# The first stage of an attention and gated-MLP kernel, written in another order: masks, transposes, product copies and weight steps

## Chip, core and metric

One core of a Trainium2 chip. The metric is device time in microseconds of one launch: 820.15 us in the median of three runs (817.03 to 821.88) for the kernel before. Engine names: TensorE (PE; PEld is its weight load), VectorE (DVE), ScalarE (ACT), GpSimd (POOL), SyncE (SP), which issues the DMAs.

## What is computed

Attention with a decay term for 8 batches of 8 heads (576 tokens, 64 per head), then a gated MLP on the joined heads:

```python
scores = scale * np.matmul(q, k.transpose(0, 1, 3, 2))
decay = cum[:, :, :, None] - cum[:, :, None, :]          # cum: running sum of log f
scores = np.where(causal, -1000000000.0, scores + decay)
attn = softmax(scores)
x = np.matmul(attn, v)                                   # heads joined: (8, 576, 512)
h = np.maximum(x @ w_in, 0.0); u, v = h[..., :512], h[..., 512:]
v_n = (v - mean) / sqrt(var + 1e-06)
out = (u * (w_spatial @ v_n + b_spatial)) @ w_out
```

## The kernel before

Two heads make a pair; a batch has four pairs (PPB = 4), there are 32 in all. Of a head's 576 query rows, four blocks of 128 are handled by head; the last 64 rows of both heads share one tile, the tail. For a pair, TensorE computes scores; DVE (`lowest`, line 279) adds the decay table, finds the row minimum and writes the weights' exponents; ACT (line 310) takes the exponential with a row sum; POOL (`share`, line 287) scales by the reciprocal; TensorE transposes the weights (line 379 by head, 389 for the tail); ACT and DVE copy the transposes out of PSUM (line 370); and TensorE multiplies them with v (line 417). That last step is called the product. Its result is split into two float32r parts: xh by ACT (line 426), xl by DVE (line 427).

The kernel has two stages. The first (`first`) does the attention of batch 0 and, beside it, brings in the weights: w_in comes as 64-bit numbers in four blocks, each going through a DMA (line 120), one ACT operation (125), five DVE operations (127 to 133), a POOL addition (135), an ACT cast (137) and a POOL subtraction (138); `go(blocks, n)` takes one of these steps. A w_spatial slice (`go(spaces, n)`) is a DMA (151), then an ACT cast (153) and a POOL subtraction (154). In the second stage the MLP of one batch runs beside the attention of the next, and a planner places its instructions; it also converts the other half of w_in and w_out.

In the first stage the order on every engine is the written one: a loop after `period` ties each instruction to the one before it on its engine. `period(P)` overlaps the scores of pair X = P + 1 with the transposes and the product of pair P, for P = -1 to 3; `y` is true from P = 0 on. `prep(P)` issues a pair's five loads on SP (q and k, the decay tables dk of both heads, the tail's tables dt); `mask(P)` is six POOL selections on these tables; `prep_v` loads v once the product before has read the old one. Scores use PSUM banks 0 to 3, the product banks 4 and 5, transposes two buffers `tp`. `leave()` finishes the product of the pair before: the xh and xl copies. `keep_warm` runs matmuls on zeros.

Of the kernel before, what the change touches and what calls it, by code (L numbers as in the profile page):

```python
# [8 lines left out]
F32 = mybir.dt.float32  # L9
# [11 lines left out]
S = 576  # L21
# [10 lines left out]
def f32(ap):  # L32
    return ap.bitcast(F32)
# [3 lines left out]
def attn_gmlp_kernel(ctx: ExitStack, tc: tile.TileContext, qk, v, f, w_in, w_sp, b_sp, w_out, out):  # L37
# [163 lines left out]

    freed, banks = {}, []

    def bank(n):

        t = PS['s'].tile([128, 512], F32, name="sc", tag=f"sc{n}")
        banks.append(n)
        return t

    def in_one_piece(jobs, needs=()):  # L210
# [37 lines left out]
    def mask(P):  # L248

        _, dk, dt = tab[P]  # L250
        for h in range(2):
            two = dk[h][:, 256:768].rearrange("p (c w) -> p c w", w=256)[:, :, 0:128]
            G.affine_select(out=two, in_=two, compare_op=ALU.is_ge, fill=-8.0 * BIG, base=0,
                            pattern=[[0, 2], [-1, 128]], channel_multiplier=1)
            G.affine_select(out=dk[h][:, 640:896].rearrange("p (c w) -> p c w", w=128),
                            in_=dk[h][:, 0:256].rearrange("p (c w) -> p c w", w=128), compare_op=ALU.is_ge,
                            fill=-8.0 * BIG, base=0, pattern=[[0, 2], [-1, 128]], channel_multiplier=1)
            p = slice(64 * h, 64 * h + 64)
            G.affine_select(out=dt[p, TL:S], in_=dt[p, TL:S], compare_op=ALU.is_ge, fill=-8.0 * BIG, base=0,
                            pattern=[[-1, 64]], channel_multiplier=1)  # L260

# [20 lines left out]
    def share(P, t, r):  # L282

        if PPB < P < 2 * PPB:
            A.activation(t, t, AF.Copy, scale=r)
        else:
            G.tensor_scalar(out=t, in0=t, scalar1=r, scalar2=1.0, op0=ALU.mult, op1=ALU.mult)  # L287
# [82 lines left out]
        copied.setdefault(P, []).append(by(out, ps))  # L370
        nev[0] += 1

    def turn_block(P, h, c, by=None):

        tt, _ = turn(P)
        n = 512 - 128 * c
        tp = PS['t'].tile([128, 512], F32, name="tp")
        for i in range(c, NB):
            T.transpose(out=tp[:, (i - c) * 128:(i - c + 1) * 128],  # L379
                        in_=tt[h][:, TOFF[i] + 128 * c:TOFF[i] + 128 * c + 128], identity=ident)  # L380
        return lambda by=None: evac(P, e_tile(P)[:, h, EOFF[c]:EOFF[c] + n], tp[:, 0:n], by)
# [26 lines left out]
    def attend(P, xh, xl):  # L408

        vt, e = vts[P], es.pop(P)  # L410
        xb = 4 if P < PPB else 0
        x0, x1 = bank(xb), bank(xb + 1)
        jobs = []

        def product(x, s0, q0, q1, c, h, end):
            e0 = EOFF[c] - 128 * c
            return lambda: T.matmul(x[64 * h:64 * h + 64, q0 - s0:q1 - s0], vt[:, c, h, :],  # L417
                                    e[:, h, e0 + q0:e0 + q1], start=c == 0, stop=c == end)

        for c in range(NB + 1):  # L420
            for x, s0, q0, q1, end in ((x1, 256, max(256, 128 * c), S, NB), (x0, 0, 128 * c, 256, 1)):
                jobs += [product(x, s0, q0, q1, c, h, end) for h in range(2) if c <= end]
        in_one_piece(jobs, copied.pop(P))
        yield 2950
        for ps, s0, n in ((x0, 0, 256), (x1, 256, 320)):
            last[P, s0 // 256] = A.copy(xh[:, s0:s0 + n], ps[:, 0:n])  # L426
            freed[xb + s0 // 256] = V.tensor_tensor(out=xl[:, s0:s0 + n], in0=ps[:, 0:n], in1=f32(xh[:, s0:s0 + n]),  # L427
                                               op=ALU.subtract)
        yield 0
# [10 lines left out]
    def first(ws):  # L440

        blocks, spaces, pending = {}, {}, []

        def leave():
            for g in pending:
                for _ in g:
                    pass
            pending.clear()

        def go(d, n):  # L450
            if n in d:
                next(d[n], None)

        def period(P):

            X = P + 1
            y = P >= 0
            qk_t, dk, dt = tab[X]
            tt, tl = turn(X)
            nm = wk.tile([128, 2, 4], F32, name="nm", tag="nm8", bufs=2)  # L460
            sa = wk.tile([128, 2, 3], F32, name="sa", tag="sa", bufs=2)
            sb = wk.tile([128, 2, 1], F32, name="sb", tag="sb", bufs=2)
            nt = wk.tile([128, 4], F32, name="nm", tag="nm", bufs=6)
            st = wk.tile([128, 4], F32, name="sm", tag="sm", bufs=6)

            def low(i, at):
                for h in range(2):
                    weigh(X, i, h, tt[h], dk[h], at, nm[:, h, i:i + 1], sb[:, h, 0:1] if i == 3 else sa[:, h, i:i + 1])

            def inverse(s_):  # L470
                V.tensor_scalar(out=s_, in0=s_, scalar1=1.0e-9, scalar2=None, op0=ALU.add)
                V.reciprocal(s_, s_)

            def spread(i, s_):
                for h in range(2):
                    t = tt[h][:, TOFF[i]:TOFF[i] + 128 * (i + 1)]
                    share(0, t, s_[:, h, 0:1])

            def two(h, c):
                if y:  # L480
                    a = turn_block(P, h, c)
                    b = turn_block(P, h, c + 1)
                    a(A.copy)
                    b(V.tensor_copy)

            at = score_piece(X, qk_t, (0, 1, 2))
            if y:
                if P + 2 <= PPB:
                    list(prep(P + 2))
                go(blocks, P + 2)  # L490
            else:
                keep_warm(6)
            low(2, at)
            leave()
            go(spaces, P)
            two(0, 0)
            low(1, at)
            go(blocks, P)
            low(0, at)
            go(blocks, X)  # L500
            two(0, 2)
            at = score_piece(X, qk_t, (3,))
            if not y:
                keep_warm(6)
            two(1, 0)
            inverse(sa)
            low(3, at)
            for i in (2, 1, 0):
                spread(i, sa[:, :, i:i + 1])
            two(1, 2)  # L510
            tails = []
            for j in range(2):
                sc = bank(2 + j)
                mm(sc[:, 0:288], qk_t[:, TL:640], qk_t[:, 640 + 288 * j:928 + 288 * j], True, True)
                tails.append(sc)
            banks.clear()
            for j in range(2):
                k0 = 288 * j
                freed[2 + j] = lowest(tl[:, k0:k0 + 288], tails[j][:, 0:288], dt[:, k0:k0 + 288], nt[:, j:j + 1])
            V.tensor_tensor(out=nt[:, 2:3], in0=nt[:, 0:1], in1=nt[:, 1:2], op=ALU.min)  # L520
            inverse(sb)
            spread(3, sb)
            A.activation(tl[:, 0:S], tl[:, 0:S], AF.Exp, bias=nt[:, 2:3], scale=-1.0, accum_out=st[:, 0:1])
            if y:
                a, b = (turn_tail(P, *k) for k in TAILS)
                a(A.copy)
                b(V.tensor_copy)
            go(blocks, X)
            inverse(st[:, 0:1])
            share(0, tl[:, 0:S], st[:, 0:1])  # L530
            if P + 2 <= PPB:
                mask(P + 2)
            go(blocks, X)
            if y:
                pending.append(product(P))
                next(pending[0])
                if X < PPB:
                    prep_v(X)
            go(spaces, X)

        for c in range(NJ):
            blocks[c] = load_first(ws, c)
        for c in range(NB + 1):
            spaces[c] = load_space(ws, c)
        traced = nc.cur_bb.bb.instructions
        start = len(traced)
        rows, qk0, qk1 = decay_rows(), prep(0), prep(1)
        next(rows)
        next(qk0)
        next(blocks[0])  # L550
        next(rows)
        next(qk0)
        prep_v(0)
        list(qk1)
        next(blocks[1])
        warm.append(PS['t'].tile([128, 512], F32, name="tp"))
        keep_warm(30)
        mask(0)
        for P in range(-1, PPB):
            period(P)  # L560
        leave()
        was = {}
        for i in list(traced)[start:]:
            if i.engine in was:
                tc.add_manual_dep(i, was[i.engine].name, mybir.DependencyInfo(
                    mybir.DependencyClass.NoSync, mybir.DependencyReason.DATA), reason="order")
            was[i.engine] = i
        go(spaces, NB)
# [210 lines left out]
```

## Time and profile before

| | |
|---|---|
| median of three runs (lowest to highest) | 820.15 us (817.03 to 821.88) |
| the profiled execution, its own time | 819.35 us |
| its span, first to last instruction | 817.2 us |
| TensorE matmul, busy | 769.7 us (94%) |
| DVE / ACT / POOL, busy | 430.5 / 417.2 / 368.1 us |
| mean granted TensorE clock | 0.974 |
| chain that ended last: TensorE's share | 69% |

The profile is of one execution. Shares over the whole span are a mean over two stages: the first ends at some 101.6 us, when TensorE starts on the MLP of batch 0. The rows below are therefore taken from stretches. Matmuls are pipelined and their ends are modelled; an idle time stands in brackets ahead of the instruction that ended it, with what released it. A clock of 1.0 is 2.4 GHz, 0.5 is 1.2 GHz.

### The profile page before, as it was taken

The page shows a single profiled execution, that of the slowest core. Times are in us where ns is not written, and L with a number is a line of the kernel's source. Part 1 is how long each engine was busy: PE and PEld are TensorE (multiplying, and loading weights), DVE is VectorE, ACT ScalarE, POOL GpSimd, SP SyncE. Part 2 cuts the span into 40 slices and gives each one's busy share as a digit, 9 for nine tenths or more (in the row PEclk, how much of TensorE's full clock was granted, in tenths as well). Part 3 has the DMA queues.
Part 4 walks back from the last instruction along what each step waited for, and adds up shares of the span by engine and source line. Part 5 has one row for each costly group of instructions (what it writes and reads, how often), then busy time and mean ns, then how long its engine had stood idle before and what let it go on. Part 6 is the DMA issues. An engine that isn't in the chain of part 4 may idle for free.

```text
span 817.2 us, 14547 instructions
## 1 busy us (share of the span) xinstructions
PE 769.7 (94%) x4922; PEld 608.2 (74%) x4922; DVE 430.5 (53%) x1502; ACT 417.2 (51%) x1127; POOL 368.1 (45%) x686
## 2 busy tenths in 40 slices
PE   6676788989999999999999999999999999999997
PEld 2344467768788877887788777888788778878896
DVE  2566779855454446545564536544464446544322
ACT  2555548775565446544564446544564446543331
POOL 1566566433544436333554436334554445433231
PEclk9689899999999999999999999999999999999999
DMA  7544434422333333222332333312332332211001
GB/s 197 166 134 139 131 112 146 134 73 80 98 94 95 120 119 93 94 60 82 115 94 94 120 107 100 96 47 92 120 95 94 120 103 72 85 31 43 27 1 65
DMA packets 34764, 79.43 MB, mean 97 GB/s; under 512 B 4225, under 2 KB 8321, under 8 KB 34690
## 3 DMA queue, kind: packets, MB, share of 16 engines
q1 hardware_dynamic: 34370, 77.98, 31.1%
q8 instruction: 39, 0.64, 0.3%
q10 hardware_dynamic: 320, 0.52, 0.2%
q14 instruction: 35, 0.29, 0.1%
HBM read 68.73 MB, written 9.75 MB: 96 GB/s over the span
## 4 chain that ended last, share of the span: by engine, by line
PE 69%; issue 5%; DVE 4%; POOL 3%; DMA 2%; ACT 2%; POOLq 0%; DVEq 0%; ACTq 0%
PE ps L226 39%; PE sc L417 8%; PE tp L379 7%; PE sc L299 7%; PE sc L226 5%; PE tp L226 2%; DMA out_dram<-o 1%; POOL gl L680 1%; PE tp L389 1%; DVE tt L279 1%; ACT tt L310 1%; POOL tt L287 1%; ACT gh L679 1%; DVE w L130 0%; DMA dt<-rows_d 0%
## 5 line engine op out<-in xcount | busy, mean ns | idle before, releaser
L310 ACT ACTIVATE tt<-tt,nm 128x128 f32<-128x128 f32 (+2 forms) x240 | 133.7, 558 | 120.5 <-DVE nm L279 118.0
L287 POOL TENSOR_SCALAR tt<-tt,sm 128x128 f32<-128x128 f32 x192 | 99.7, 537 | 110.8 <-DVE sm L326 110.8
L379 PE MATMUL tp<-ident,tt 128*128 128x128 f32 x600 | 113.9, 287 | 15.1 <-DVE e L370 8.2
L379 PEld LDWEIGHTS tp<-ident,tt 128*128 128x128 f32 x600 | 76.3, 143 | 55.1 <-issue 11.5
L680 POOL TENSOR_TENSOR gl<-u,gh 128x256 fp32r<-128x256 f32 (+1 forms) x64 | 51.5, 805 | 142.3 <-ACT gh L679 140.1
L299 PE MATMUL sc<-qk_t 64*128 64x128 f32 (+3 forms) x512 | 91.5, 477 | 8.7 <-DVE nm L279 8.7
L417 PE MATMUL sc<-e,vraw 128*64 128x320 f32 (+4 forms) x896 | 93.6, 360 | 4.8 <-ACT e L370 3.3
L279 DVE CUSTOM_DVE_ANT_1 tt<-sc,dk 128x256 f32<-128x256 f32 (+1 forms) x120 | 65.7, 551 | 58.3 <-PE sc L299 43.8
L370 DVE COPY e<-tp 128x384 f32<-128x384 f32 (+1 forms) x160 | 71.0, 444 | 36.8 <-PE tp L379 29.5
L417 PEld LDWEIGHTS sc<-e,vraw 128*64 128x64 f32 x896 | 59.9, 137 | 40.5 <-ACT e L370 4.2
L370 ACT COPY e<-tp 128x256 f32<-128x256 f32 (+1 forms) x160 | 72.4, 453 | 32.6 <-PE tp L379 29.4
L226 PE MATMUL ps<-sph,vnh 128*128 128x256 f32 (+1 forms) x240 | 75.7, 315 | 0.7 <-DVE u L676 0.7
L226 PE MATMUL ps<-xh,winh 128*128 128x256 f32 (+1 forms) x232 | 74.2, 320 | 0.0
L226 PE MATMUL ps<-spl,vnh 128*128 128x256 f32 (+1 forms) x240 | 71.4, 297 | 0.0
L226 PE MATMUL ps<-sph,vnl 128*128 128x256 f32 (+1 forms) x240 | 71.1, 296 | 0.0
L226 PE MATMUL ps<-xh,winl 128*128 128x256 f32 (+1 forms) x232 | 70.8, 305 | 0.0
L279 DVE CUSTOM_DVE_ANT_0 tt<-sc,dk 128x128 f32<-128x128 f32 (+1 forms) x120 | 50.1, 420 | 37.5 <-PE sc L299 15.3
L299 PEld LDWEIGHTS sc<-qk_t 64*128 64x128 f32 x512 | 45.3, 191 | 32.6 <-issue 16.4
L226 PE MATMUL ps<-xl,winh 128*128 128x256 f32 (+1 forms) x232 | 69.6, 300 | 0.0
L427 DVE TENSOR_TENSOR xl<-sc,xh 128x256 fp32r<-128x256 f32 x64 | 28.3, 454 | 74.0 <-ACT xh L426 73.9
L226 PE MATMUL ps<-winh,xh 128*128 128x512 f32 x148 | 63.1, 427 | 2.2 <-ACT o L704 1.7
L226 PE MATMUL ps<-winl,xh 128*128 128x512 f32 x148 | 58.6, 397 | 0.0
(191 smaller groups left out, 1720.8 us busy)
## 6 DMA issues: line engine op xcount, KB each, us to landing
qk_t<-in_dram SPq DMA_DIRECT2D x32, 608.0 KB, 5.4
dk<-rows_d SPq DMA_DIRECT2D x60, 320.0 KB, 4.4
vraw<-in_dram SPq DMA_DIRECT2D x32, 320.0 KB, 3.0
dt<-rows_d SPq DMA_DIRECT2D x60, 144.0 KB, 4.3
out_dram<-o SPq DMA_DIRECT2D x32, 256.0 KB, 2.1
w<-in_dram SPq DMA_DIRECT2D x16, 256.0 KB, 2.8
w<-in_dram SPq DMA_DIRECT2D x4, 512.0 KB, 7.7
d<-rows_d SPq DMA_DIRECT2D x4, 320.0 KB, 7.5
```

The costliest lines, as they stand in the source:

```text
L226: T.matmul(o, l, r, start=st, stop=sp)
L279: return V.tensor_tensor_reduce(out=out, in0=ps, in1=dec, scale=-0.125, scalar=3.0e38, op0=ALU.add, op1=ALU.min, accum_out=acc_)
L287: G.tensor_scalar(out=t, in0=t, scalar1=r, scalar2=1.0, op0=ALU.mult, op1=ALU.mult)
L299: return lambda: T.matmul(ps[:, c:c + n], qk_t[p, n - 128:n], qk_t[p, 640:640 + n], start=True, stop=True)
L310: last["exp", P, h, i] = A.activation(t, t, AF.Exp, bias=nm, scale=-1.0, accum_out=sm)
L370: copied.setdefault(P, []).append(by(out, ps))
L379: T.transpose(out=tp[:, (i - c) * 128:(i - c + 1) * 128], in_=tt[h][:, TOFF[i] + 128 * c:TOFF[i] + 128 * c + 128], identity=ident)
L389: T.transpose(out=tp[:, j * 128:(j + 1) * 128], in_=tl[:, c * 128:(c + 1) * 128], identity=ident)
L417: return lambda: T.matmul(x[64 * h:64 * h + 64, q0 - s0:q1 - s0], vt[:, c, h, :], e[:, h, e0 + q0:e0 + q1], start=c == 0, stop=c == end)
L427: freed[xb + s0 // 256] = V.tensor_tensor(out=xl[:, s0:s0 + n], in0=ps[:, 0:n], in1=f32(xh[:, s0:s0 + n]), op=ALU.subtract)
L679: A.copy(gh[j][:, 0:nt], g)
L680: G.tensor_tensor(out=gl[j][:, 0:nt], in0=g, in1=f32(gh[j][:, 0:nt]), op=ALU.subtract)
```

## The change

Only the first stage is rewritten. `mask(X + 1)` is called in the middle of a period instead of at its end, and its two selections on the tail's tables come last. A head's four blocks of transposes are issued together, blocks 2 and 3 into banks 4 and 5 (the product's) instead of the two `tp` buffers. The product's finishing is split: the two xh casts come first in a period, the xl subtractions after the six score passes of blocks 2, 1 and 0. The copies of the transposes are dealt out to ACT and DVE anew, the sums' reciprocals come after block 3's passes, the loads of the next pair move from a period's start to behind the tail's passes, and the w_in steps stand around the product. Block 0 of w_in is converted before the first period, and twelve warming matmuls go.

```diff
--- before.py
+++ after.py
@@ -201,10 +201,11 @@
 
     freed, banks = {}, []
 
-    def bank(n):
+    def bank(n, piece=True):
 
         t = PS['s'].tile([128, 512], F32, name="sc", tag=f"sc{n}")
-        banks.append(n)
+        if piece:
+            banks.append(n)
         return t
 
     def in_one_piece(jobs, needs=()):
@@ -255,7 +256,7 @@
             G.affine_select(out=dk[h][:, 640:896].rearrange("p (c w) -> p c w", w=128),
                             in_=dk[h][:, 0:256].rearrange("p (c w) -> p c w", w=128), compare_op=ALU.is_ge,
                             fill=-8.0 * BIG, base=0, pattern=[[0, 2], [-1, 128]], channel_multiplier=1)
-            p = slice(64 * h, 64 * h + 64)
+        for p in (slice(0, 64), slice(64, 128)):
             G.affine_select(out=dt[p, TL:S], in_=dt[p, TL:S], compare_op=ALU.is_ge, fill=-8.0 * BIG, base=0,
                             pattern=[[-1, 64]], channel_multiplier=1)
 
@@ -370,11 +371,11 @@
         copied.setdefault(P, []).append(by(out, ps))
         nev[0] += 1
 
-    def turn_block(P, h, c, by=None):
+    def turn_block(P, h, c):
 
         tt, _ = turn(P)
         n = 512 - 128 * c
-        tp = PS['t'].tile([128, 512], F32, name="tp")
+        tp = bank(2 + c, False) if P < PPB and c > 1 else PS['t'].tile([128, 512], F32, name="tp")
         for i in range(c, NB):
             T.transpose(out=tp[:, (i - c) * 128:(i - c + 1) * 128],
                         in_=tt[h][:, TOFF[i] + 128 * c:TOFF[i] + 128 * c + 128], identity=ident)
@@ -424,6 +425,8 @@
         yield 2950
         for ps, s0, n in ((x0, 0, 256), (x1, 256, 320)):
             last[P, s0 // 256] = A.copy(xh[:, s0:s0 + n], ps[:, 0:n])
+        yield 0
+        for ps, s0, n in ((x0, 0, 256), (x1, 256, 320)):
             freed[xb + s0 // 256] = V.tensor_tensor(out=xl[:, s0:s0 + n], in0=ps[:, 0:n], in1=f32(xh[:, s0:s0 + n]),
                                                op=ALU.subtract)
         yield 0
@@ -471,43 +474,49 @@
                 V.tensor_scalar(out=s_, in0=s_, scalar1=1.0e-9, scalar2=None, op0=ALU.add)
                 V.reciprocal(s_, s_)
 
-            def spread(i, s_):
+            def spread(i, s_, by_a=False):
                 for h in range(2):
                     t = tt[h][:, TOFF[i]:TOFF[i] + 128 * (i + 1)]
-                    share(0, t, s_[:, h, 0:1])
-
-            def two(h, c):
-                if y:
-                    a = turn_block(P, h, c)
-                    b = turn_block(P, h, c + 1)
-                    a(A.copy)
-                    b(V.tensor_copy)
-
+                    share(PPB + 1 if by_a else 0, t, s_[:, h, 0:1])
+
+            def turned(h):
+                return [turn_block(P, h, c) for c in range(NB)] if y else [lambda by: None] * NB
+
+            def step(n):
+                for g in pending:
+                    for _ in range(n):
+                        next(g, None)
+
+            VC, AC = V.tensor_copy, A.copy
+
+            step(1)
             at = score_piece(X, qk_t, (0, 1, 2))
-            if y:
-                if P + 2 <= PPB:
-                    list(prep(P + 2))
-                go(blocks, P + 2)
-            else:
-                keep_warm(6)
             low(2, at)
-            leave()
+            c0 = turned(0)
             go(spaces, P)
-            two(0, 0)
+            c0[0](AC)
             low(1, at)
             go(blocks, P)
+            c0[2](AC)
             low(0, at)
-            go(blocks, X)
-            two(0, 2)
+            step(2)
+            pending.clear()
+            c0[1](VC)
+            c0[3](VC)
+            if y and X < PPB:
+                mask(X + 1)
             at = score_piece(X, qk_t, (3,))
-            if not y:
-                keep_warm(6)
-            two(1, 0)
+            c1 = turned(1)
+            c1[0](AC)
+            low(3, at)
             inverse(sa)
-            low(3, at)
+            c1[1](VC)
+            c1[2](AC)
+            c1[3](VC)
             for i in (2, 1, 0):
                 spread(i, sa[:, :, i:i + 1])
-            two(1, 2)
+            if not y:
+                mask(1)
             tails = []
             for j in range(2):
                 sc = bank(2 + j)
@@ -518,24 +527,30 @@
                 k0 = 288 * j
                 freed[2 + j] = lowest(tl[:, k0:k0 + 288], tails[j][:, 0:288], dt[:, k0:k0 + 288], nt[:, j:j + 1])
             V.tensor_tensor(out=nt[:, 2:3], in0=nt[:, 0:1], in1=nt[:, 1:2], op=ALU.min)
-            inverse(sb)
-            spread(3, sb)
-            A.activation(tl[:, 0:S], tl[:, 0:S], AF.Exp, bias=nt[:, 2:3], scale=-1.0, accum_out=st[:, 0:1])
+            if X + 2 <= PPB:
+                list(prep(X + 2))
+            if X:
+                go(blocks, X + 1)
             if y:
                 a, b = (turn_tail(P, *k) for k in TAILS)
-                a(A.copy)
-                b(V.tensor_copy)
-            go(blocks, X)
-            inverse(st[:, 0:1])
-            share(0, tl[:, 0:S], st[:, 0:1])
-            if P + 2 <= PPB:
-                mask(P + 2)
-            go(blocks, X)
+                a(VC)
+                b(VC)
+            if X:
+                go(blocks, X)
+            inverse(sb)
+            spread(3, sb, not y)
+            A.activation(tl[:, 0:S], tl[:, 0:S], AF.Exp, bias=nt[:, 2:3], scale=-1.0, accum_out=st[:, 0:1])
+            if X:
+                go(blocks, X)
             if y:
                 pending.append(product(P))
                 next(pending[0])
                 if X < PPB:
                     prep_v(X)
+            inverse(st[:, 0:1])
+            if X:
+                go(blocks, X)
+            share(0, tl[:, 0:S], st[:, 0:1])
             go(spaces, X)
 
         for c in range(NJ):
@@ -550,12 +565,15 @@
         next(blocks[0])
         next(rows)
         next(qk0)
+        list(qk1)
         prep_v(0)
-        list(qk1)
         next(blocks[1])
         warm.append(PS['t'].tile([128, 512], F32, name="tp"))
         keep_warm(30)
+        for _ in range(3):
+            go(blocks, 0)
         mask(0)
+        go(blocks, 0)
         for P in range(-1, PPB):
             period(P)
         leave()
```

## Rows read from the trace of the kernel before

**Rows 1.** Busy us (instructions) per engine by stretch; then PEclk (granted clock), DMA share, GB/s.

```profile
47.13:65.22 18.09, 13.03 (x75) 8.03 (x75) 11.18 (x42) 9.67 (x28) 10.89 (x18) 0.81 0.51 151
...
83.09:101.62 18.53, 13.24 (x74) 8.06 (x74) 13.10 (x48) 11.38 (x32) 11.13 (x20) 0.82 0.52 136
...
120.00:140.00 20.00, 17.39 (x111) 14.00 (x112) 18.23 (x57) 16.87 (x45) 13.40 (x21) 0.91 0.39 128
...
160.00:817.20 657.20, 647.46 (x4244) 527.39 (x4240) 321.59 (x1149) 327.06 (x882) 279.93 (x531) 1.00 0.27 85
...
52.00:58.80 6.80, 5.78 (x18) 3.15 (x19) 3.08 (x16) 4.35 (x14) 2.78 (x3) 0.51 0.80 205
```

**Rows 2.** TensorE's timeline, one period: start us, us, engine, line, op, tiles, [idle before <-releaser].

```profile
47.05 1.57 PE L299 MATMUL sc<-qk_t 64*128 64x384 f32 x12
...
52.62 0.90 PE L379 MATMUL tp<-ident,t 128*128 128x128 f32 x3 [3.08 <-ACT e L370]
...
53.89 2.08 PE L299 MATMUL sc<-qk_t 64*128 64x512 f32 x4 [0.37 <-DVE nm L279]
...
62.30 2.92 PE L417 MATMUL sc<-e,vraw 128*64 128x320 f32 x28 [0.70 <-ACT e L370]
```

**Rows 3.** The same view of POOL, DVE and ACT after the product's end at 47.13.

```profile
47.57 0.74 POOL L287 TENSOR_SCALAR tl<-tl,sm 128x576 f32<-128x576 f32 x1 [2.62 <-DVE sm L472]
...
48.71 0.56 DVE L279 CUSTOM_DVE_ANT_0 tt<-sc,dk 128x384 f32<-128x384 f32 x1 [1.30 <-POOL dk L253]
...
50.33 1.26 POOL L135 TENSOR_TENSOR w<-w,wa 128x512 f32<-128x512 f32 x1
...
50.83 0.68 ACT L426 CAST xh<-sc 128x256 fp32r<-128x256 f32 x2
...
51.40 0.68 ACT L153 CAST sph<-wraw 128x576 fp32r<-128x576 f32 x1
...
53.10 0.51 ACT L310 ACTIVATE tt<-tt,nm 128x256 f32<-128x256 f32 x1 [0.54 <-DVE nm L279]
...
55.39 0.65 ACT L125 ACTIVATE wa<-w 128x512 f32<-128x512 f32 x1
...
55.95 0.35 ACT L370 COPY e<-tp 128x256 f32<-128x256 f32 x1
```

**Rows 4.** SP's queue in that period; then its DMAs: count, KB each, us to landing.

```profile
47.17 0.34 SPq L264 DMA_DIRECT2D vraw<-in_dram  x1
...
47.56 0.42 SPq L151 DMA_DIRECT2D wraw<-in_dram  x1
...
50.66 0.74 SPq L120 DMA_DIRECT2D w<-in_dram  x1
...
w<-in_dram SPq DMA_DIRECT2D x1, 512.0 KB, 7.7
...
wraw<-in_dram SPq DMA_DIRECT2D x1, 288.0 KB, 3.4
```

**Rows 5.** The same view of DVE from the sums' reciprocals to the tail's copy.

```profile
58.17 0.16 DVE L471 TENSOR_SCALAR sa<-sa 128x6 f32<-128x6 f32 x1
...
58.47 0.65 DVE L279 CUSTOM_DVE_ANT_1 tt<-sc,dk 128x512 f32<-128x512 f32 x1
...
59.66 0.29 DVE L370 COPY e<-tp 128x128 f32<-128x128 f32 x1
...
60.73 0.16 DVE L520 TENSOR_TENSOR nm<-nm 128x1 f32<-128x1 f32 x1
...
61.64 0.56 DVE L370 COPY e<-tp 128x384 f32<-128x384 f32 x1 [0.27 <-PE tp L389]
```

**Rows 6.** The start: TensorE's warming matmuls, SP's loads for pair 2, DVE's first pass.

```profile
22.61 2.41 PE L226 MATMUL tp<-zm 128*128 128x512 bf16 x6
...
26.02 0.33 SPq L233 DMA_DIRECT2D qk_t<-in_dram  x1
...
32.08 0.56 DVE L279 CUSTOM_DVE_ANT_0 t<-sc,d 128x384 f32<-128x384 f32 x1 [1.30 <-DMA dk<-rows_d]
```

## The prediction

> **What bounds the kernel now.** Three views in this order: busy time by stretch, TensorE's own timeline through one period, then all engines there. The stretches [rows 1] show two regimes. From 160 us on TensorE is busy 647 of 657 us and the first stage cannot touch that. Before 101.6 us the kernel runs periods of some 18 us (18.09 and 18.53) in which no engine is full: TensorE 13.0, DVE 11.2, ACT 9.7, POOL 10.9 us. So the first stage is a chain of waits in queues whose order is written by hand, and what a new order is worth is read from that chain. TensorE's rows [rows 2]: one product gives way to the next scores at 47.05 (its own end is put at 47.13), the following one starts at 62.30 and ends at 65.22; between them TensorE stands still for 3.08 us before the transposes at 52.62, and after that stop the clock is granted at half, 0.51 from 52.0 to 58.8 [rows 1], 1.2 instead of 2.4 GHz; the scores of block 3 at 53.89 take 2.08 us there.
>
> Why the stop [rows 3]: POOL scales the tail's weights at 47.57, then masks pair 2's tables (six instructions, until POOL's next work at 50.33, some 2.0 us). DVE's first score pass at 48.71 has waited 1.30 us for the first mask. ACT comes to the product's copy only at 50.83, 3.7 us after the product ended, to the weight cast at 51.40, and then to the copy that gives TensorE a transpose buffer back. There are two such buffers, so the other transposes of the head stand behind it. Everything later in the period hangs on this: the second head's first copy is behind the first head's last.
>
> **The change part by part.** Let t = 0 be the end of a product on TensorE, T the period, and w the moment at which the period's w_spatial slice has landed.
>
> Masks: the six POOL instructions (2.0 us) move from between two periods to the middle, ahead of the three scalings; they serve the next pair. The score pass no longer waits for them: it loses the 1.30 us. POOL works 10.9 us in 18.1, so at T = 14 to 16 it still has room; the price is that the scalings of blocks 2, 1 and 0 start up to 2 us later, under the next product, and are needed only at the next transposes. Taken as nothing; if that cover goes, 2 us a period.
>
> Four banks: a head's ten transposes no longer wait for copies; blocks 2 and 3 of the transposes go to the product's banks, so they wait for DVE's subtraction of the old product, which now comes after all six score passes, at t = 3 to 4 (the first scores' 1.57 us, then passes of at most the 0.56 us at 48.71, the first of them beside the scores). Behind that wait TensorE's queue holds the scores of block 3 and the second head. That is still earlier than the 53.89 - 47.13 = 6.8 of before. The 3.08 us stop goes.
>
> Product's result first: two ACT casts ahead of the exponentials; they are 0.6 us on ACT (50.83 to 51.40) [rows 3] and free nothing by themselves, since the subtraction sits later.
>
> w_in steps: DVE's five bit operations stay behind the tail copies, under the product; ACT's first step (0.65 us at 55.39) leaves the middle of the period. POOL's addition for the block goes with them. Before, they delayed the tail's scaling and so the masks; now they delay at most the next first score pass. The DMA for the next w_in block moves too, see below. Block 0's work goes ahead of the first period, where DVE and POOL were idle. In that period ACT also takes two scalings from POOL, before the tail's exponential; they are off the path, which is POOL's other six.
>
> What is late next is in SP's queue. The five table and q/k loads moved from the head of a period to behind its tail scores, and the w_in load with them. Behind these now stand v and the w_spatial slice, and the cast of that slice is early in ACT's queue: the first head's first copy, four exponentials, the w_in cast and two copies stand behind it. Before, the slice was second in an empty queue: issued 0.4 us after v at 47.17, landed 3.4 us later, so w = 3.8 [rows 4]. From that v to the landing of the last of the six loads is 50.66 + 7.7 - 47.17 = 11.2 us [rows 4], which is what the set needs in one queue. The new order issues the same set from about T - 5.0 (still to come then: 1.1 for the tail's passes and minimum, as from 59.66 to 60.89 [rows 5], 0.9 for two copies, 0.1 of handover, 2.92 of product), so the slice, now last, lands at T - 5.0 + 11.2, that is w = 6.2 in the next period. The ends are w = 3.8 (nothing in front of it) and w = 6.2 (strictly in turn). The rows show loads landing in the order of issue, so I take a value near the upper end.
>
> The Trainium skill, "DMA: Bandwidth & Descriptors", section "Queues, rings and completion order", says that each DMA engine takes descriptors in ring order but that completion is not first in, first out for an issuing engine. By the first half w is 6.2 and by a loose reading of the second it could come near 3.8; the landings of this trace (3.4 for the second load, 7.7 for the sixth) speak for the first.
>
> From w to the product: ACT's chain from the cast at 51.40 to the copy at 55.95 is 4.55 us; without the wait of 0.54 and the moved 0.65, and with the last copy's 0.35, 3.7 [rows 3]. Then DVE's: from the reciprocal group at 58.17 to the minimum's end at 60.73 + 0.16 is 2.7, less the 1.2 of block 3's two passes (58.47 to 59.66), which the new order does earlier, plus the copies of 0.56 (second head), 0.35 and 0.56 (tail): 3.0 [rows 5]. Then the product, 2.92, and 0.3 for three handovers. Together 9.9: T = w + 9.9, between 13.7 and 16.1. I take 15.4 for the two periods behind a full set of loads and 14.3 for the last one (no tables, no w_in behind period 2, so w = 3.8, plus 0.6 for the bias parts, as 18.53 is longer than 18.09).
>
> The start. Warming matmuls (2.41 us at 22.61) go, a table's mask no longer stands behind the tail's table (1.0 taken for it), so the tail scores end and the load at 26.02 issues some 3.4 us earlier, at 22.6 [rows 6]; the set behind it needs about 10 us (no v, but the rest of a w_in block ahead of it), so the first slice lands at 32.6. The first score pass of pair 1 could start some 5 us before its 32.08 [rows 6], but the slice decides: the first product ends at 32.6 + 9.9 - 0.6 (no w_in cast) = 41.9 instead of 47.1, a gain of 5.2. Without the queue it would be 7.5.
>
> Sum: 41.9 + 2 x 15.4 + 14.3 = 87.0 for the end of the last product, against 101.6: 14.6 us. The second stage follows as it is. Its first part is not TensorE's alone (DVE 18.23 of 20 us from 120 to 140 [rows 1], by the rest of the w_in conversion), but that work starts from the end of the first stage too. The profiled execution took 819.35 us (span 817.2): 804.8. It lies 0.8 under the median of three, so for the median I say 805.
>
> **The rivals.** Slice early: w stays near 3.8 in each period. Then T = 13.7 in all three and the first product ends at 39.5: 80.6, a gain of 21, 798. For it: the DMA engines are busy 0.51 of a period [rows 1]. Against: landing in turn, as above. Range 795 to 800.
>
> Given back: the second stage's start is set by DVE and POOL converting w_in's other half, not by TensorE. If those loads and tiles come no earlier than they do by the first stage's loads, half of the gain stays there: 812, 811 to 817. For it: 18.23 of 20 us. Against: the tiles they use are freed by the first stage's end.
>
> The order does not bind, the loads do: were w 8 us or more, T is again 18 and only the start's gain is left, 814 to 820.
>
> Slower: the clock. TensorE now waits at two places in a period, between block 3's scores and the first copy behind the slice (t = 5.2 to about w + 1.2), and before the third transposes. If such a stop brings the half clock, as the 3.08 us stop did, and it now lasts until the product, the product costs 2.9 us more and the next six scores 1.6 more (1.57 at the full clock), 4.5 a period in four periods: 18 us, 805 + 18 = 823. It decides from where the stop reaches the 3 us of [rows 2]; at w = 6.2 it is 2.2 us. The warming matmuls that go make it likelier at the start.
>
> **How the numbers follow.** Chances: forecast 0.55 (own range 800 to 810), slice early 0.16, given back 0.12, loads bind 0.08, clock 0.09. The range leaves out the clock case, the worst of the two before it and the best of the early slice: 797 to 813. 0.5% is 4.1 us, about what a measurement of this kernel can tell from no change, so faster is under 816.0: 0.55 + 0.16 + 0.10 + 0.02 = 0.83; same 0.08; slower 0.09.
>
> **What would show it.** Right: the first product into the second stage's first bank at 84 to 91 us; TensorE's stops inside a period under 2.5 us and the clock at 1.0 through most of periods 1 to 3; DVE's first score pass waiting for the scores and not for POOL; ACT's longest wait of a period at the w_spatial cast, released by its DMA. Wrong: that cast without a wait (slice early), a period of 18 us with the same wait (loads bind), the half clock over a product (clock), or a shorter first stage with TensorE idle more than 5 us longer between its end and 60 us after it (given back).

## The result

The changed kernel takes 810.76 us in the median of four runs (809.26 to 812.48), the kernel before 819.36 (817.03 to 821.88): a ratio of 0.9895, 95% interval 0.9858 to 0.9932. That is 8.6 us faster, inside the range of 797 to 813; the forecast was 14.6 and 805. The forecast's own range of 800 to 810 is missed by 0.8 us. The profiled execution took 812.48 us (span 810.7); it is the slowest of the four and has the lowest mean clock, 0.968 against 0.974 to 0.981 in the others.

Busy time of the changed kernel by stretch (columns as in [rows 1]): its three periods, the second stage, and a piece of the first period.

```profile
42.90:60.92 18.02, 12.05 (x75) 8.36 (x75) 12.02 (x41) 9.40 (x27) 10.96 (x18) 0.81 0.52 156
...
60.92:77.28 16.36, 12.91 (x76) 8.62 (x75) 12.25 (x42) 9.41 (x27) 11.65 (x20) 0.79 0.44 135
...
77.28:94.33 17.05, 13.29 (x74) 9.16 (x74) 11.94 (x43) 9.96 (x28) 12.22 (x19) 0.80 0.62 178
...
94.33:810.70 716.37, 701.51 (x4569) 569.65 (x4568) 380.62 (x1309) 368.10 (x992) 313.21 (x581) 0.99 0.29 89
...
52.00:54.00 2.00, 1.99 (x10) 1.59 (x9) 0.00 (x0) 2.00 (x10) 1.44 (x2) 0.50 0.00 0
```

The first stage ends at 94.33 us instead of 101.62, and the second takes 716.4 us, against 715.6 before. Between the two profiled executions lie 6.9 us: 7.3 gained in the first stage, 0.8 lost behind it, and 0.4 around the span. But the periods last 18.0, 16.4 and 17.1 us where 15.4, 15.4 and 14.3 were forecast, and their clock is 0.79 to 0.81, no better than in [rows 1].

TensorE's timeline of the changed kernel (as [rows 2]): the period from the first product's end at 42.90, and the last product.

```profile
42.83 1.57 PE L300 MATMUL sc<-qk_t 64*128 64x384 f32 x12
...
46.51 0.70 PE L380 MATMUL sc<-ident,t 128*128 128x128 f32 x3 [1.20 <-DVE xl L430]
...
51.69 1.75 PE L380 MATMUL tp<-ident,t 128*128 128x128 f32 x7 [3.43 <-ACT e L371]
...
54.15 1.96 PE L227 MATMUL sc<-qk_t 128*128 128x288 f32 x4
...
58.00 2.92 PE L418 MATMUL sc<-e,vraw 128*64 128x320 f32 x28 [1.34 <-ACT tl L542]
...
89.72 4.61 PE L418 MATMUL sc<-e,vraw 128*64 128x320 f32 x28 [2.16 <-ACT tl L542]
```

The stop of 3.08 us ahead of the first head's third transposes [rows 2] is now 1.20, for DVE's subtraction, as planned. A stop of 3.43 us stands ahead of the second head's transposes instead; the clock there is 0.50 (52.00 to 54.00, the last of the stretches above), and the tail scores behind it take 1.96 us, against 1.19 at 58.57 in the kernel before. What ended that stop is in ACT's queue, the same view; all casts of a w_spatial slice are shown.

```profile
32.48 0.67 ACT L153 CAST sph<-wraw 128x576 fp32r<-128x576 f32 x1 [3.58 <-DMA wraw<-in_dram]
...
50.48 0.67 ACT L153 CAST sph<-wraw 128x576 fp32r<-128x576 f32 x1 [4.70 <-DMA wraw<-in_dram]
...
51.06 0.58 ACT L371 COPY e<-tp 128x512 f32<-128x512 f32 x1
...
66.83 0.67 ACT L153 CAST sph<-wraw 128x576 fp32r<-128x576 f32 x1 [2.57 <-DMA wraw<-in_dram]
...
80.97 0.67 ACT L153 CAST sph<-wraw 128x576 fp32r<-128x576 f32 x1 [0.36 <-DMA wraw<-in_dram]
```

The cast waits 3.58, 4.70 and 2.57 us for its DMA, 0.36 in the last period. The copy at 51.06, which gives TensorE a transpose buffer back, stands right behind the cast: 51.06 + 0.58 is the end of the stop. SP's queue shows why the slice is late:

```profile
38.10 0.34 SPq L234 DMA_DIRECT2D qk_t<-in_dram  x1
...
40.63 0.53 SPq L120 DMA_DIRECT2D w<-in_dram  x1
...
42.93 0.34 SPq L265 DMA_DIRECT2D vraw<-in_dram  x1
...
43.32 0.42 SPq L151 DMA_DIRECT2D wraw<-in_dram  x1
```

The set for the pair after next is issued from 38.10 on, v and the slice last, at 42.93 and 43.32. The slice lands 7.2 us after its issue (50.48 - 43.32), and 5.5 in the next period (66.83 - 61.35), against 3.4 in the kernel before [rows 4]. So w = 50.48 - 42.90 = 7.6 us in this period, 5.9 in the next (66.83 - 60.92), and 3.7 in the last.

DVE (two rows of the same period) confirms the masks' part and shows who waits now:

```profile
43.87 0.56 DVE L280 CUSTOM_DVE_ANT_0 tt<-sc,dk 128x384 f32<-128x384 f32 x1
...
54.22 0.31 DVE L474 TENSOR_SCALAR sa<-sa 128x6 f32<-128x6 f32 x1 [4.61 <-ACT tt L311]
```

The first score pass starts without its wait for POOL [rows 3]; DVE comes to it from its own w_in steps and a reciprocal (43.69 + 0.16). The reciprocals wait 4.61 us for ACT's exponentials, which are behind the slice's cast.

### The profile page after: what moved, and what is told of

It reads as the page before. It is cut to its first block, busy times and chain, and to the rows that moved or that the text cites. A ratio compares the mean times of both kernels' runs of the same rounds, so it can differ in the third digit from the quotient of the medians.

```text
span 810.7 us, 14511 instructions
## 1 busy us (share of the span) xinstructions
PE 768.0 (95%) x4910; PEld 612.4 (76%) x4910; DVE 438.7 (54%) x1506; ACT 416.9 (51%) x1125; POOL 367.4 (45%) x684
## 4 chain that ended last, share of the span: by engine, by line
PE 73%; issue 2%; ACT 2%; DMA 2%; DVE 2%; POOL 1%; SPq 0%; POOLq 0%; DVEq 0%; ACTq 0%
PE ps L227 41%; PE sc L418 8%; PE sc L300 7%; PE tp L380 7%; PE sc L227 5%; PE tp L227 2%; DMA out_dram<-o 2%; PE tp L390 1%; ACT tt L311 1%; DVE tt L280 1%; POOL tt L288 0%; ACT tt L286 0%; DMA dt<-rows_d 0%; ACT o L722 0%; POOL gl L698 0%
## 5 line engine op out<-in xcount | busy, mean ns | idle before, releaser
L380 PE MATMUL tp<-ident,tt 128*128 128x128 f32 x588 | 105.3, 286 | 8.8 <-ACT e L371 5.1
L380 PEld LDWEIGHTS tp<-ident,tt 128*128 128x128 f32 x588 | 74.1, 144 | 40.4 <-issue 11.7
L418 PE MATMUL sc<-e,vraw 128*64 128x320 f32 (+4 forms) x896 | 95.3, 364 | 5.9 <-ACT tl L542 5.4
L371 ACT COPY e<-tp 128x256 f32<-128x256 f32 (+1 forms) x148 | 67.7, 457 | 40.0 <-PE tp L380 37.4
L371 DVE COPY e<-tp 128x384 f32<-128x384 f32 (+2 forms) x156 | 70.0, 451 | 28.0 <-PE tp L380 14.2
```

Source lines behind the costliest of these rows:

```text
L380: T.transpose(out=tp[:, (i - c) * 128:(i - c + 1) * 128], in_=tt[h][:, TOFF[i] + 128 * c:TOFF[i] + 128 * c + 128], identity=ident)
```

## Experiments

The theory: a period lasts w + 9.9 us, and w is set by what is queued ahead of the slice on SP. The rivals: the moved loads cost nothing and another edit holds the periods at 16 to 18 us; or the half clock does.

**Is it the slice's place in the queue?** Three kernels. The first is the changed kernel with the slice's step ahead of the pair's loads:

```diff
             V.tensor_tensor(out=nt[:, 2:3], ...)
+            go(spaces, X)
             if X + 2 <= PPB:
                 list(prep(X + 2))
...
             share(0, tl[:, 0:S], st[:, 0:1])
-            go(spaces, X)
```

> The changed kernel, with one edit: the load of a w_spatial slice is issued ahead of the next pair's five loads instead of behind them and the v load. Theory Q (the slice's place in SP's queue is the new wait): ACT's cast of the slice no longer waits (it waited 3.6, 4.7, 2.6 and 0.4 us in the changed kernel), the periods of pairs 1 and 2 fall from 18.0 and 16.4 to about 14, the first period's end from 42.9 to about 39.5, the last product ends at 82 to 86 instead of 94.3, and the time is 799 to 803. Rival C (the chain on ACT and DVE behind the cast, or TensorE's half clock, holds the period anyway): the periods stay at 16 us or more, the last product ends at 91 or later, 807 or more.

Measured: 800.56 us (799.88 to 802.57), ratio 0.9767 (0.9737 to 0.9797). Its issue of a slice (SP), the cast of that slice (ACT), and its periods:

```profile
38.83 0.45 SPq L151 DMA_DIRECT2D wraw<-in_dram  x1
```

```profile
54.26 0.66 ACT L153 CAST sph<-wraw 128x576 fp32r<-128x576 f32 x1
```

```profile
38.40:51.27 12.87, 10.07 (x76) 6.94 (x75) 12.53 (x43) 9.17 (x27) 10.57 (x17) 1.00 0.71 222
...
51.27:64.30 13.03, 10.08 (x76) 6.94 (x75) 12.72 (x42) 9.17 (x27) 12.07 (x20) 1.00 0.52 159
...
64.30:79.98 15.68, 10.56 (x75) 6.83 (x74) 11.77 (x42) 9.95 (x28) 12.49 (x19) 1.00 0.56 157
```

The slice is now issued right behind the v of the product before, 15 us ahead of its cast, which no longer waits. It is still behind a set on SP and takes 6.8 us to land (5.1 the next time); what the edit gives it is a period's lead. The periods are 12.9, 13.0 and 15.7 us, the clock is 1.00 in all of them, and the first stage ends at 79.98. That is earlier than the 82 to 86 expected; the prediction's rival "slice early" had 80.6 for that end and 798 for the time.

The second kernel makes the opposite trial: the kernel before, with nothing but these loads moved to where the change puts them.

```diff
-            if y:
-                if P + 2 <= PPB:
-                    list(prep(P + 2))
-                go(blocks, P + 2)
-            else:
+            if not y:
                 keep_warm(6)
...
             V.tensor_tensor(out=nt[:, 2:3], ...)
+            if X + 2 <= PPB:
+                list(prep(X + 2))
+            if X:
+                go(blocks, X + 1)
```

> The kernel before, with one part of the change alone: the next pair's five loads and the next w_in block's load are issued behind the tail's passes instead of at a period's head. Theory Q: the slice lands 6 to 7.5 us after a product instead of 3.8, the cast waits 2 to 3 us in the periods of pairs 1 and 2, the last product ends 4 to 6 us later than 101.6, and the time is 823 to 826 against 819.4. Rival C: the old order's cast comes late enough (4.3 us after the product) and its chain is bound by the transpose buffers, so the time stays within 2 us of 819.4.

Measured: 822.03 us, ratio 1.0035 (1.0020 to 1.0049). Two of its casts (ACT), and TensorE's stops in the same periods:

```profile
54.66 0.67 ACT L153 CAST sph<-wraw 128x576 fp32r<-128x576 f32 x1 [1.46 <-DMA wraw<-in_dram]
...
74.46 0.67 ACT L153 CAST sph<-wraw 128x576 fp32r<-128x576 f32 x1 [2.01 <-DMA wraw<-in_dram]
```

```profile
55.87 0.90 PE L379 MATMUL tp<-ident,t 128*128 128x128 f32 x3 [4.83 <-ACT e L370]
...
75.67 0.90 PE L379 MATMUL tp<-ident,tt 128*128 128x128 f32 x3 [5.25 <-ACT e L370]
```

The kernel before had no such wait in the period of [rows 3], and a small one in the next:

```profile
69.95 0.67 ACT L153 CAST sph<-wraw 128x576 fp32r<-128x576 f32 x1 [0.28 <-DMA wraw<-in_dram]
```

The stops of some 3 us become 4.83 and 5.25, and the first stage ends at 105.78. The move alone costs 4.2 us there, as expected, and 2.9 in the total (822.03 against 819.11), less than the 823 to 826 expected.

The third is the changed kernel with the loads back at a period's head, behind v and the slice:

```diff
             at = score_piece(X, qk_t, (0, 1, 2))
+            if y:
+                if P + 2 <= PPB:
+                    list(prep(P + 2))
+                go(blocks, P + 2)
...
-            if X + 2 <= PPB:
-                list(prep(X + 2))
-            if X:
-                go(blocks, X + 1)
```

> The changed kernel, with one part undone: the next pair's five loads and the next w_in block's load are issued at a period's head again, behind the w_spatial slice, as before the change. Theory Q: the slice lands 3.7 to 4 us after a product as before, the tables land 6.7 to 10 us after it, in time for the masks in the middle; periods of 13.8 to 14.5 us, last product's end at 82 to 86 instead of 94.3, time 800 to 804. Rival T (the tables' late landing now holds the masks and the scalings behind them on POOL): periods of 16 us or more, end at 90 or later, 807 or more.

Measured: 796.70 us (796.37 to 797.48), ratio 0.9733 (0.9712 to 0.9754), the fastest version here. Two casts (ACT), a mask of the second period (POOL) and the last product (PE):

```profile
41.90 0.67 ACT L153 CAST sph<-wraw 128x576 fp32r<-128x576 f32 x1 [0.77 <-DMA wraw<-in_dram]
...
55.49 0.67 ACT L153 CAST sph<-wraw 128x576 fp32r<-128x576 f32 x1 [0.99 <-DMA wraw<-in_dram]
```

```profile
61.00 0.41 POOL L254 TENSOR_SCALAR_AFFINE_SELECT dk<-dk 128x256 f32<-128x256 f32 x1 [1.44 <-DMA dk<-rows_d]
```

```profile
78.03 4.49 PE L418 MATMUL sc<-e,vraw 128*64 128x320 f32 x28 [2.17 <-ACT tl L542]
```

Here w = 41.90 - 38.20 = 3.7 and 55.49 - 51.56 = 3.9; the periods are 13.36 and 13.64 us, so T - w is 9.7 in both. The last period, with the bias parts and a product at half the clock for most of its 4.49 us, lasts 17.3 us (65.20 to 82.52). The masks wait up to 1.44 us for their tables, which does not show in the periods. The time is below the 800 to 804 expected. So the changed order without its load move is worth 22 us, and the move takes 14 of them back, 11.8 of these in the first stage (94.33 - 82.52).

**Is it the clock?** Twelve matmuls on zeros, issued between block 3's scores and the second head's transposes, fill the stop:

```diff
             at = score_piece(X, qk_t, (3,))
+            tails = [bank(2), bank(3)]
+            banks.clear()
+            if y:
+                for _ in range(12):
+                    mm(tails[0], zm[:, 0:128], zm[:, 0:512], True, True)
             c1 = turned(1)
```

> The changed kernel, with twelve matmuls on zeros put into TensorE's stop between block 3's scores and the second head's transposes, into a bank that is free then; the order of all else stays. Theory H (the half clock after that stop is what makes a period end later than the slice's landing by 10.4 instead of 9.9 us, and what makes the last product take 4.6 us): the tail's scores take 1.2 us instead of 2.0, 0.5 us a period, and the last product 2.9; end at 90 to 92 instead of 94.3, time 807 to 809. Rival W (only the slice's landing counts): the end stays within 1 us of 94.3.

Measured: 812.15 us (810.32 to 814.55), ratio 0.9916 (0.9893 to 0.9940). Its periods:

```profile
41.41:57.12 15.71, 12.70 (x87) 8.01 (x87) 11.71 (x43) 9.28 (x27) 10.20 (x16) 1.00 0.60 180
...
57.12:73.74 16.62, 12.91 (x86) 7.92 (x87) 11.56 (x42) 9.27 (x27) 12.06 (x20) 1.00 0.40 125
...
73.74:89.82 16.08, 12.46 (x86) 8.09 (x86) 12.81 (x44) 10.06 (x29) 12.82 (x20) 1.00 0.53 159
```

The clock is 1.00, yet the periods last 15.7, 16.6 and 16.1 us: its casts still wait (3.10 and 4.01 us in the first two, w = 6.0 and 7.0), and T - w is 9.7. In the changed kernel it is 10.4 in each of its first two periods. The half clock there costs 0.7 us a period, then, not the period itself. The first stage ends 4.5 us earlier, at 89.82, but the time is not the 807 to 809 expected; it is not told apart from the changed kernel's. The first 300 us of the second stage, in the changed kernel and then in this one:

```profile
94.33:394.33 300.00, 290.61 (x1872) 231.55 (x1872) 180.70 (x618) 170.28 (x466) 137.56 (x252) 0.98 0.33 102
```

```profile
89.82:389.82 300.00, 284.70 (x1829) 226.84 (x1830) 173.86 (x600) 166.03 (x451) 137.53 (x249) 0.98 0.33 101
```

TensorE is busy 290.6 us in one (1872 matmuls) and 284.7 in the other (1829): some 6 us more of idle time, at no lower a clock. This is the kind of loss that the prediction's rival "given back" names, although its mark, more than 5 us within the first 60, is not reached (51.10 us busy there, against 53.91 in the kernel before and 54.80 in the changed one). The second stage's instructions also stand in another order in each version, and whether that order or the converted weights hold it was not separated. Nor is all of the 4.5 us the filling's, as the small edits show below.

**Are the four banks needed?** The changed kernel with all transposes in the two `tp` buffers, and the kernel before with only the banks edit:

```diff
-        tp = bank(2 + c, False) if P < PPB and c > 1 else PS['t'].tile([128, 512], F32, name="tp")
+        tp = PS['t'].tile([128, 512], F32, name="tp")
```

> The changed kernel, with one part undone: all transposes of the first stage go through the two transpose buffers again. Theory Q: the third transposes of the first head then wait for ACT's first copy, which stands behind the cast of the slice, and block 3's scores wait behind them; that adds 1.0 to 1.5 us a period, the last product ends at 97 to 100, time 813 to 817. Rival B (the four banks are where the gain came from): all of the 7.3 us of the first stage go, the end is at 101 or later, 818 or more.

> The kernel before, with one part of the change alone: transposes of blocks 2 and 3 go to the product's two banks; the written order stays. Theory P (the parts work only together): the third transposes then wait for the subtractions at 52.07 instead of the copy at 52.6, and the second head's first transposes for ACT's first copy instead of its third; 0.8 to 1.5 us a period, last product's end at 96 to 98 instead of 101.6, time 813 to 816. Rival B (the banks carry the gain by themselves, as the two-buffer run suggests with its 9.7 us): end at 94 or earlier, 812 or less.

Measured: 821.45 us, ratio 1.0018 (0.9995 to 1.0040), and 820.58 us, ratio 1.0015 (0.9991 to 1.0039). TensorE in the first, then in the second:

```profile
54.48 0.90 PE L380 MATMUL tp<-ident,t 128*128 128x128 f32 x3 [7.10 <-ACT e L371]
```

```profile
52.05 0.70 PE L380 MATMUL sc<-ident,t 128*128 128x128 f32 x3 [2.25 <-DVE xl L428]
...
54.24 2.08 PE L300 MATMUL sc<-qk_t 64*128 64x512 f32 x4 [1.50 <-DVE nm L280]
```

With two buffers the first head's third transposes wait for the copy behind the slice's cast, and block 3's scores and the second head stand behind them: a stop of 7.10 us. The edit is worth 10.7 us in the changed kernel (821.45 - 810.76), more than theory Q had (813 to 817): the time is the one that rival B gave, 818 or more. But B's reason, that the banks carry the gain by themselves, falls with the second run. Alone they are worth nothing: the old order puts the subtraction, and the score passes that wait for the masks, where the copies were, so a stop of 3.08 becomes 2.25 and 1.50. Both times expected of that run, 813 to 816 and 812 or less, were missed.

**Are the masks free?** `mask(X + 1)` moved back to a period's end, in the changed kernel and in the one with the slice first:

```diff
-            if y and X < PPB:
-                mask(X + 1)
...
-            if not y:
-                mask(1)
...
             share(0, tl[:, 0:S], st[:, 0:1])
+            if X < PPB:
+                mask(X + 1)
```

> The changed kernel, with one part undone: the masks stand at the end of a period again, behind the tail's scaling. Theory Q: the first score pass starts some 2.3 us later, but where the cast of the slice waits to 5.9 or 7.6 us after the product that is hidden; only the last period, where the slice lands at 3.7 us, pays about 2 us: end at 94 to 97, time 811 to 814. Rival M (the masks hold the period): 1.3 to 2.3 us in each of four periods, end at 100 or later, 816 to 820.

> The version with the slice's load first, and the masks at a period's end again. In the changed kernel that cost nothing (810.3 against 810.8), and by theory Q only because the slice's wait hid it. Theory Q: with that wait gone the first score pass starts 2 to 2.3 us later in each of three or four periods (12.9 us each now), the last product ends at 86 to 88 instead of 80.0, time 806 to 809. Rival N (the masks' place never matters): end at 80 to 81.5, time 800 to 802.

Measured: 810.27 us, ratio 0.9880 (0.9844 to 0.9917), and 812.26 us, ratio 0.9928 (0.9905 to 0.9950). DVE's first score pass in the one and in the other, and TensorE in the other:

```profile
63.62 0.56 DVE L280 CUSTOM_DVE_ANT_0 t<-sc,d 128x384 f32<-128x384 f32 x1 [2.21 <-POOL d L254]
```

```profile
60.13 0.56 DVE L280 CUSTOM_DVE_ANT_0 t<-sc,d 128x384 f32<-128x384 f32 x1 [2.21 <-POOL d L254]
```

```profile
63.01 0.88 PE L380 MATMUL sc<-ident,tt 128*128 128x128 f32 x3 [3.61 <-DVE xl L430]
```

The same wait of 2.21 us costs nothing where the slice comes later anyway, and 11.7 us in all (812.26 - 800.56) where it doesn't: the subtraction stands behind the score passes, and the transposes in the product's banks wait 3.61 us for it. The time is above the 806 to 809 expected: the three periods last 16.3, 17.3 and 17.2 us, and the clock in them is 0.90, 0.80 and 0.80, where it was 1.00 with the slice first alone.

**The small edits.** The product's two ACT casts put behind the first two exponentials, the first ACT step of w_in put back in mid period, and, with the slice first, the last slice and the bias parts put behind the last product:

```diff
-            step(1)
             at = score_piece(X, qk_t, (0, 1, 2))
             low(2, at)
+            step(1)
...
             low(0, at)
+            if X:
+                go(blocks, X)
             step(2)
...
                 b(VC)
-            if X:
-                go(blocks, X)
...
         leave()
+        go(spaces, NB)
...
-        go(spaces, NB)
```

> The changed kernel, with one part undone: the product's two ACT casts stand behind the first two exponentials instead of ahead of them. Theory Q: DVE's subtraction comes only after six score passes and the casts are long done by then, so nothing waits: end at 94 to 95, time 810 to 812. Rival F (the casts first are what lets the banks be free early): 1 us or more a period, end at 98 or later, 814 or more.

> The changed kernel, with one part undone: ACT's first step of a w_in block (0.65 us) stands in the middle of a period again, behind the last exponentials of blocks 2, 1 and 0. Theory Q: the step lies on the chain from the slice's cast to the product, 0.56 us in each of three periods, end at 95.5 to 96.5, time 811 to 813. Rival O (it lies behind the reciprocals' release and costs nothing): end within 0.5 us of 94.3.

> The version with the slice's load first, and the last w_spatial part and the bias rows (two ACT casts, two DVE subtractions) put behind the last product instead of inside the last period, which is 15.7 us long against 12.9 and 13.0 for the two before it. Theory Q: that period falls to 13 to 13.5, the last product ends at 77.5, and as the second stage needs those parts late the time is 797 to 799. Rival G (the second stage gives back: its start is set by the w_in conversion on DVE, which these operations now delay): the end is as early, but the time stays at 800 to 803.

Measured: 812.76 us (0.9929, 0.9901 to 0.9957), 809.63 (0.9890, 0.9863 to 0.9917) and 800.19 (0.9790, 0.9758 to 0.9822). The times of the first two are not told apart from the changed kernel's. Their first stages end at 90.6 and 91.4 us, though, earlier than any end expected of them. The first six scores of pair 1 in the changed kernel and in the one with the casts late, and the last product of the latter:

```profile
24.00 2.93 PE L300 MATMUL sc<-qk_t 64*128 64x384 f32 x12 [0.67 <-DVE nm L280]
```

```profile
23.59 1.57 PE L300 MATMUL sc<-qk_t 64*128 64x384 f32 x12 [0.74 <-DVE nm L280]
...
87.68 2.93 PE L418 MATMUL sc<-e,vraw 128*64 128x320 f32 x28 [2.23 <-ACT tl L542]
```

Up to the first product the order written in the two kernels is the same, and yet that product ends at 42.90 in one and at 41.34 in the other: the clock differs between the executions that were profiled. With the 1.7 us of a last product mostly at half the clock, the end of a first stage is known from one profile to some 3 us only, and of the 4.5 us of the filled stop it stays open how much is the filling's.

In the third the last period is 13.0 us instead of 15.7, so the bias parts cost 2.7 us there, and the first stage ends 2.2 us earlier (77.79 against 79.98). The total is not told apart from that of the slice first alone (800.56), but its four runs go from 798.88 to 804.75, so whether the 2.2 us were given back is open.

## Why the prediction was right, and where its sizes were off

**The new wait** was named: the w_spatial cast on ACT, held by its DMA behind the moved set. The three kernels on the load order show it from both sides. With it the time came into the range, but the periods came out nearer to a rival's than to the forecast's: "loads bind" had 18 us from w = 8 on, and the first full period has 18.0 with w = 7.6.

**w, the slice's landing,** was the largest miss in the middle. The working gave 6.2 as the upper end and took 5.5 with T = 15.4; measured were 7.6 and 5.9. The set's 11.2 us (from one period of [rows 4]) was 50.48 - 38.10 = 12.4 and 66.83 - 56.15 = 10.7 here. This is the term that was too small. The upper end of the range was not one: it rested on a single sample, and a value below it was chosen although the rows spoke for strictly in turn. Why the set took 12.4 us once and 10.7 the next time was not looked into.

The Trainium skill, "DMA: Bandwidth & Descriptors", section "Queues, rings and completion order", was read two ways in the prediction. In the traces of the kernel before, the changed one, the slice first and the loads at the head, the landings that the profile shows come in the order of issue, which agrees with its half on ring order; no run shows the slice overtaking the set.

**From w to the product,** 9.9 us: 9.7 at the full clock (the loads at the head, the filled stop), 10.4 in the changed kernel's two full periods, with half the clock behind the stop. A good sum, less the clock.

**The stop of 3.08 us** did not go, it moved. The rival on the clock had the place right (between block 3's scores and the first copy behind the slice) and the formula, w + 1.2: with w = 7.6 that is 8.8 after the product's end, at 51.7, and TensorE restarted at 51.69. It had the price wrong: the clock was back before the product in the full periods (2.92 us at 58.00), so it cost 0.7 and not 4.5. Its condition, a stop of 3 us, was wrong as well. In the last period of the changed kernel no stop is longer than 1.59 us before the clock falls:

```profile
81.28 0.70 PE L380 MATMUL sc<-ident,t 128*128 128x128 f32 x3 [1.59 <-DVE xl L430]
...
82.97 1.65 PE L380 MATMUL tp<-ident,t 128*128 128x128 f32 x7
```

The seven transposes took 0.98 us at 44.33. And a stop of 2.28 us ahead of the last product left it at 2.92 us with the slice first, while 2.17 us ahead of it went with 4.49 us with the loads at the head:

```profile
77.06 2.92 PE L418 MATMUL sc<-e,vraw 128*64 128x320 f32 x28 [2.28 <-ACT tl L543]
```

So the length of one stop does not tell here whether the clock falls.

**The last period,** 14.3, took 17.05 with w as forecast (3.7). Two terms were missed. The product ran at half the clock for most of its 4.61 us, instead of 2.92; in the executions with the casts late and with the w_in step in mid period it did not, and this period took 15.3 and 15.7. And the bias parts, taken at 0.6 from two periods that differ by 0.44 (18.53 - 18.09), stand between score passes on DVE:

```profile
84.24 1.36 DVE L163 TENSOR_TENSOR sptb<-wraw,spta 64x576 fp32r<-64x576 f32 x1 [0.47 <-ACT spta L162]
...
87.07 0.81 DVE L165 TENSOR_TENSOR bs<-br,bs 1x576 fp32r<-1x576 f32 x1
```

**The start** was right to 1.0 us: the slice's cast at 32.48 (32.6 forecast), the first product's end at 42.90 (41.9). This 1.0 is within what the clock of one execution makes of it (42.90 and 41.34 above).

**Masks at nothing** was right only under the cover that the text named; without it they cost more than the 2 us a period that it gave: 11.7 us in all, with a lower clock in it.

The misses add up: 1.0 at the start, 2.6 and 1.0 in the two full periods, 2.75 in the last make 7.3, which is 14.6 less the 7.3 that the first stage gained. Of what would have shown the forecast right, two signs came true in part: the score pass no longer waits for POOL (it waits for DVE's own queue, not for the scores), and ACT's longest wait is the one for the slice in the three periods behind a set, but not in the last (0.36 us). The product's end (84 to 91), stops under 2.5 us and the clock near 1.0 did not come. Two signs of being wrong did, each once: a period of 18 us with the same wait ("loads bind"), the first, and the half clock over most of a product ("clock"), the last.

## What to carry to other kernels

When a hand-written order moves loads, write out the DMA queue as a list and see which small load with an early reader ends up behind the set; issuing it a period ahead, or leaving the set where it was, was worth 10 to 14 us of this change's 22. A cost that is hidden by a wait is not zero: price it again as soon as the wait is gone, and test edits together, since here the banks gave nothing alone and 10.7 us with the rest. A stage that ends earlier is only a gain if the next one can start on it: with the filled stop the first stage ended 4.5 us earlier and TensorE stood idle some 6 us longer in the 300 us behind it. And the end of a stage in one profile is one sample: here the first product's end alone moved by 1.6 us between two executions with the same instructions up to it.

## What was unexpected

The clock at half speed behind a stop of 3.43 us cost a period 0.7 us only, since TensorE is busy 12.05 of its 18.02 us; a last product mostly at that clock cost 1.7. The clock also fell behind a stop of 1.59 us. The same 288 KB load took 3.4 us behind one load and 7.2 us behind a set. And TensorE's clock went from 0.8 to 1.00, in all three periods, by moving one DMA issue, with no matmul added.
